# Decay attention, SwiGLU and maxout on one core: the place of a weight's high half in the queues of ScalarE and GpSimd

## The chip, the cores and the metric

The kernel runs on one core of one Trainium2 chip. The metric is the device time of one execution in microseconds (us). The kernel before has a median of 540.08 us over three runs (539.41 to 540.44).

## The reference, cut to what matters

Block-wise linear attention with a decay per head makes x, with 1536 rows of 512. A gated layer and a maxout layer follow. The weights of the two layers are the operands that the change is about.

```python
def _moe_ref(x, w_gate, w_val, w_out, rms_g):
    rms = np.sqrt(np.mean(x * x, axis=-1, keepdims=True) + 1e-06)
    xn = x / rms * rms_g
    g = xn @ w_gate
    silu = g * (1.0 / (1.0 + np.exp(-g)))
    return (silu * (xn @ w_val) @ w_out).astype(np.float32)

def _moe2_ref(x, w1, w2, w3, w_out):
    h = np.maximum(np.maximum(x @ w1, x @ w2), x @ w3)
    return (h @ w_out).astype(np.float32)
```

w_gate, w_val and w_out (512 x 1536, 1536 x 512) arrive as 64-bit floats, and the chip turns them into 32-bit floats itself.

## The kernel before, in words

Every product of the two layers is made of three matmuls: an operand is split into a high half (`xh`, `wh`, `hh`: the value rounded to the type that TensorE reads) and a low half (`xl`, `wl`, `hl`: the value less its high half), and high by high, high by low and low by high are added in PSUM.

The attention runs over 12 chunks of 128 rows. After the first chunks its steps are put between the matmuls of the first layer: transposes of keys and queries (`turn`, L297 and L299) that ScalarE copies out (kT L301, qT L303), scores (L326, with the state's products on L331), mixed values (px L384), their squares (sq L395), a row sum on VectorE (L401), the division by the norm (x L425), the high half of x (xh L427), its low half on GpSimd (xl L435), and a power of -1/2 on GpSimd (diag L414).

A **unit** is one 128x512 slice of a weight matrix: g (gate), v (value) or o (output), with its number. A unit takes three **thirds** for its 32-bit words and then its two halves:

- `begin_unit`: ScalarE makes the absolute high words (L252) and the scaled low words (L253).
- `words_of_unit` 0 to 2: VectorE clamps (L209), masks and shifts (L212) and puts the sign back (L216); GpSimd then adds the low words (L219). Now the tile W holds the 32-bit weight.
- `finish_unit`: ScalarE rounds W to `wh` (L180), GpSimd subtracts to `wl` (L183).

`third_of_unit` (L257) runs one third per call. In a round of three calls it carries one unit's words and finishes the unit before it (`done`): the finish stands in the second call. The matmul loops call it from `spread` and `gap`, after every three matmuls or so.

The **plain part** is the first four slices of the inner dimension, where each product is formed directly (`hidden1`, `out_two`). It runs as long as the list `lates` is empty; `spread` fills that list once the attention has ended. After that comes a part with fewer products, sums of weights and a third call that closes a sum (`later`).

In the plain part the units stand in this order: g0, v0, g1, v1, g2, o0, o1, v2, g3, v3, o2, o3. In the built program the W tiles of those that matter here are numbered W_809 (v1), W_887 (g2), W_958 (o0), W_1037 (o1), W_1176 (v2), W_1229 (g3), W_1376 (v3), W_1426 (o2) and W_1572 (o3).

Each engine takes its instructions in the order in which this code writes them. TensorE's order is that of the matmul loops; a matmul waits for its operands, and those behind it wait with it. SyncE issues the loads.

Of the kernel before, what the change touches and what calls it, by code (L numbers as in the profile page):

```python
# [26 lines left out]
def tile_decay_attention_swiglu_maxout(  # L27
# [41 lines left out]
    lates = []  # L69
# [86 lines left out]
    stage1, stage2 = [], []  # L156
# [17 lines left out]
    def finish_unit(key, W, at):  # L174
        if key:
            if second_sum(key):
                W = sums_in.pop((key[0][1], key[1]))
            wh = wpools[at].tile([P, 512], F32R, tag="wh", name="wh")
            wl = wpools[at].tile([P, 512], F32R, tag="wl", name="wl")
            nc.scalar.copy(out=wh, in_=W.bitcast(F32))  # L180
            if second_sum(key):
                return lambda: lower_of_sum(key, W, wh, wl)
            nc.gpsimd.tensor_tensor(out=wl, in0=W.bitcast(F32), in1=wh.bitcast(F32), op=ALU.subtract)  # L183
            units[key] = (wh, wl)

    def first_sum(key):
        return key and (key[0] == "Tg" or key[0] != "Tv" and key[0][0] == "T" and key[1] % 2 == 0)

    def second_sum(key):
        return key[0][0] == "T" and not first_sum(key)  # L190

    def partner(key):
        return ("v", key[1]) if key[0] == "Tg" else (key[0][1], key[1] + 1)

    def lower_of_sum(key, W, wh, wl):
        nc.vector.tensor_tensor(out=wl, in0=W.bitcast(F32), in1=wh.bitcast(F32), op=ALU.subtract)
        units[key] = (wh, wl)

    def sum_bank(key):
        other = partner(key)  # L200
        sums_in[other] = psum.tile([P, 512], I32, tag="bank", name="tsum")
        nc.scalar.copy(out=sums_in[other].bitcast(F32), in_=words[other].bitcast(F32))

    def words_of_unit(n, key, W, at, lo, hi, split_add=False):

        if key and lo is not None:
            if n == 0:
                mid[key] = W if pos["narrow"] else psum.tile([P, 512], I32, tag="bank", name="mid")
                nc.vector.tensor_scalar(out=mid[key].bitcast(F32), in0=W.bitcast(F32), scalar1=LEAST, scalar2=MOST,  # L209
                                        op0=ALU.max, op1=ALU.min)  # L210
            elif n == 1:
                nc.vector.tensor_scalar(out=mid[key], in0=mid[key], scalar1=0x07FFFFFF, scalar2=3,  # L212
                                        op0=ALU.bitwise_and, op1=ALU.logical_shift_left)
            else:
                if n == 2:
                    nc.vector.scalar_tensor_tensor(out=W, in0=hi, scalar=-0x40000000, in1=mid.pop(key),  # L216
                                                   op0=ALU.bitwise_and, op1=ALU.bitwise_or)
                if n == 3 or not split_add:
                    nc.gpsimd.tensor_tensor(out=W, in0=W, in1=lo, op=ALU.add)  # L219
        elif first_sum(key):  # L220
            if n == 0:
                sum_bank(key)
                return
            a, b = W.bitcast(F32), sums_in[partner(key)].bitcast(F32)
            kept = words[partner(key)].bitcast(F32)
            todo = ((a[:, :HF], b[:, :HF], a[:, :HF]), (b[:, :HF], b[:, HF:], kept[:, :HF]),
                    (b[:, HF:], b[:, HF:], a[:, :HF]), (a[:, HF:], a[:, HF:], b[:, HF:]))
            for o, x, y in todo[2 * n - 2:2 * n]:
                nc.vector.tensor_tensor(out=o, in0=x, in1=y, op=ALU.subtract)

    def begin_unit():
        if pos["made"] == len(unit_list):
            return
        key = unit_list[pos["made"]]
        at = group_of[key] % 2
        if first_use[key] <= pos["step"] + 6 and at < len(wpools) and (key is None or room[at]):
            pos["made"] += 1
            if key is None:
                stage1.append((None,) * 5)
                return  # L240
            room[at] -= 1
            held[key] = at
            if key[0][0] == "T":
                stage1.append((key, None if second_sum(key) else words[key[0][1], key[1]], at, None, None))
                return
            load_to(min(pos["raw"] + 3, 3 * PLAIN + 1) if pos["half"] and not lates else pos["raw"] + (3 if lates else 1))
            pos["raw"] += 1
            t = raws.pop(key).rearrange("p k (f w) -> p (k f) w", w=2)
            lo, hi = t[:, :, 0], t[:, :, 1]
            W = wp.tile([P, 512], I32, tag="W", name="W", bufs=4)  # L250
            words[key] = W
            nc.scalar.activation(out=W.bitcast(F32), in_=hi.bitcast(F32), func=AF.Abs)  # L252
            nc.scalar.activation(out=lo, in_=lo.bitcast(U32), func=AF.Copy, scale=2.0 ** -29)  # L253
            stage1.append((key, W, at, lo, hi))
# [3 lines left out]
    def third_of_unit():  # L258

        if not thirds:  # L260
            if pos["seam"] and stage1 and first_sum(stage1[0][0]):
                return
            done = stage2.pop(0) if stage2 else (None,) * 3
            unit = stage1.pop(0) if stage1 else (None,) * 5
            later = []
            thirds.extend([lambda: (begin_unit(), words_of_unit(0, *unit)),
                           lambda: (later.append(finish_unit(*done)), words_of_unit(1, *unit)),
                           lambda: (later[0] and later[0](), words_of_unit(2, *unit), stage2.append(unit[:3]))])
        thirds.pop(0)()

    xh, xl = {}, {}
# [181 lines left out]
    def gap():  # L453


        pos["gap"] += 1
        if not pos["quiet"]:
            if lates and (pos["step"] == len(steps) or pos["gap"] % 4):
                third_of_unit()
        due.sort(key=lambda e: e[0])  # L460
        while due and due[0][0] <= pos["gap"]:
            due.pop(0)[1]()
        spread()
# [3 lines left out]
    def spread():  # L467
        pos["half"] += 1
        if not lates and (pos["half"] - 1) % 5 % 3:
            third_of_unit()  # L470
        if gaps[0]:
            left = sum(1 for p in attn_q if p[0] <= gaps[1])
            for _ in range(-(-left // gaps[0])):
                attn_step()
            gaps[0] -= 1
            if not attn_q and not lates:
                att_ctx.close()
                wpools.append(ctx.enter_context(tc.tile_pool(name="wp2", bufs=8)))
                lates.append(ctx.enter_context(tc.tile_pool(name="late", bufs=1)))
                pos["narrow"] = False  # L480
                x_sums()
        if pos["half"] == 1:
            finish_unit(*stage2.pop(0))
            words_of_unit(3, *split_unit[0])
# [242 lines left out]
    def unit(at, d):  # L727

        g, i = at
        if i is None:  # L730
            key = ("g", "v", "Tg", "Tv")[d], g
        else:
            key = ("T" if d > 1 else "") + "123"[i], 2 * g + d % 2
        for _ in range(60):
            if key not in units:
                third_of_unit()
        left[key] = left.get(key, (4, 3, 2, 2)[d]) - 1
        if not left[key]:
            mine = units[key]
            free(key)  # L740
            return mine
        return units[key]
# [311 lines left out]
```

## Time and profile before

| what | value |
|---|---|
| median of three runs | 540.08 us |
| the profiled execution's own time | 540.09 us |
| its span, first to last instruction | 538.3 us |
| TensorE matmul busy | 527.4 us, 98% |
| VectorE busy | 370.7 us, 69% |
| GpSimd busy | 301.5 us, 56% |
| ScalarE busy | 279.0 us, 52% |
| mean granted TensorE clock | 0.996 |

All times below are counted from the span's start. The 1.8 us between the span and the execution's time lie around the program. The first attention steps take the stretch up to about 36 us, the plain part of the first layer lies from there to about 161 us, the rest of that layer reaches to about 350 us, and the maxout layer to the end. The weights of the four slices are made before 94 us.

### The profile page before, as it was taken

How to read it: one execution, taken by the hardware profiler on the slowest of the kernel's cores; microseconds unless marked ns; L12 is line 12 of the kernel's file. 1: busy time of each engine (PE TensorE's matmuls, PEld its weight loads, DVE VectorE, ACT ScalarE, POOL GpSimd, SP SyncE). 2: the span in 40 equal slices, each digit the busy share in tenths (PEclk: the TensorE clock that was granted, in tenths of full speed). 3: DMA queues.
4: the chain of work that ended last, by engine and by line, in shares of the span. 5: the costliest groups of instructions: out<-in, count | busy, mean ns of one | idle time of the engine just before them, and what ended most of it. 6: DMA issues, size and time to landing. Idle time of an engine off the chain costs nothing.

```text
span 538.3 us, 9767 instructions
## 1 busy us (share of the span) xinstructions
PE 527.4 (98%) x3728; PEld 435.7 (81%) x3728; DVE 370.7 (69%) x680; ACT 279.0 (52%) x541; POOL 301.5 (56%) x247
## 2 busy tenths in 40 slices
PE   8998999999999999999999999999999999999997
PEld 7776777788888888888888888888888888888886
DVE  5886886549856677857667776878785587684354
ACT  3786774453553774365455446465466745641120
POOL 2487878334345666457365557985387544951060
PEclk9999999999999999999999999999999999999999
DMA  8989563001112213213131221212023321300014
GB/s 194 235 235 251 152 158 81 1 1 39 40 40 79 78 44 113 79 39 89 60 89 39 80 78 40 80 39 64 29 66 120 116 76 43 108 10 0 1 50 185
DMA packets 65598, 44.67 MB, mean 83 GB/s; under 512 B 40080, under 2 KB 61840, under 8 KB 65552
## 3 DMA queue, kind: packets, MB, share of 16 engines
q1 hardware_dynamic: 64848, 44.05, 28.6%
q8 instruction: 29, 0.48, 0.4%
q14 instruction: 17, 0.14, 0.1%
q10 hardware_dynamic: 704, 0.01, 0.1%
HBM read 40.90 MB, written 3.15 MB: 82 GB/s over the span
## 4 chain that ended last, share of the span: by engine, by line
PE 88%; POOL 4%; issue 3%; DMA 2%; DVE 2%; ACT 1%; POOLq 0%; ACTq 0%; DVEq 0%
PE p L691 34%; PE acc L882 9%; PE r L691 9%; PE acc L488 6%; PE acc L489 6%; PE acc L490 6%; PE pv L498 5%; PE q L691 4%; PE pg L498 4%; PE px L384 2%; POOL W L219 1%; DMA wraw<-in_moe_w_val_dram 1%; POOL kd L287 1%; PE pm L410 1%; PE sc L331 1%
## 5 line engine op out<-in xcount | busy, mean ns | idle before, releaser
L183 POOL TENSOR_TENSOR wl<-W,wh 128x512 fp32r<-128x512 f32 x77 | 101.5, 1319 | 51.4 <-ACT wh L180 51.4
L219 POOL TENSOR_TENSOR W<-W,wraw 128x512 int32<-128x512 int32 x60 | 78.9, 1315 | 77.8 <-DVE W L216 77.6
L180 ACT CAST wh<-W 128x512 fp32r<-128x512 f32 x77 | 47.7, 620 | 74.5 <-POOL W L219 73.0
L509 POOL TENSOR_TENSOR hl<-sg,hh 128x512 fp32r<-128x512 f32 x36 | 48.5, 1348 | 38.7 <-ACT hh L508 38.7
L691 PE MATMUL p<-xl,wh 128*128 128x512 f32 x148 | 57.6, 389 | 0.0
L691 PE MATMUL p<-xh,wh 128*128 128x512 f32 x148 | 57.6, 389 | 0.0
L691 PE MATMUL p<-xh,wl 128*128 128x512 f32 x148 | 57.6, 389 | 0.0
L488 PE MATMUL acc<-hh,wh 128*128 128x512 f32 x144 | 56.7, 394 | 0.0
L489 PE MATMUL acc<-hl,wh 128*128 128x512 f32 x144 | 56.2, 390 | 0.0
L490 PE MATMUL acc<-hh,wl 128*128 128x512 f32 x144 | 56.2, 390 | 0.0
L846 DVE TENSOR_TENSOR acc_sb<-acc,acc_sb 128x512 f32<-128x512 f32 x46 | 31.8, 690 | 17.4 <-PE acc L490 16.1
L252 ACT ACTIVATE W<-wraw 128x512 f32<-128x512 f32 x60 | 40.3, 671 | 4.4 <-DMA wraw<-in_moe_w_dram 3.3
L209 DVE TENSOR_SCALAR mid<-W 128x512 f32<-128x512 f32 x58 | 39.7, 685 | 3.3 <-ACT W L252 3.3
L212 DVE TENSOR_SCALAR mid<-mid 128x512 int32<-128x512 int32 x58 | 40.2, 694 | 0.8
L216 DVE SCALAR_TENSOR_TENSOR W<-wraw,mid 128x512 int32<-128x512 int32 x58 | 39.5, 680 | 1.0
L253 ACT ACTIVATE wraw<-wraw 128x512 int32<-128x512 uint32 x60 | 40.0, 666 | 0.0
L746 ACT COPY c<-p 128x512 f32<-128x512 f32 x34 | 19.9, 586 | 38.0 <-PE p L691 37.9
L509 POOL TENSOR_TENSOR hl<-m,hh 128x512 fp32r<-128x512 f32 x18 | 24.2, 1350 | 23.0 <-ACT hh L508 22.9
L508 ACT CAST hh<-sg 128x512 fp32r<-128x512 f32 x36 | 22.3, 620 | 26.3 <-DVE sg L632 18.7
L691 PE MATMUL p<-yh,wh 128*128 128x512 f32 x90 | 35.0, 389 | 0.0
L691 PE MATMUL p<-yl,wh 128*128 128x512 f32 x90 | 35.0, 389 | 0.0
L691 PE MATMUL p<-yh,wl 128*128 128x512 f32 x90 | 35.0, 389 | 0.0
(176 smaller groups left out, 1315.0 us busy)
## 6 DMA issues: line engine op xcount, KB each, us to landing
wraw<-in_moe_w_out_dram SPq DMA_DIRECT2D x18, 512.0 KB, 3.4
wraw<-in_moe_w_dram SPq DMA_DIRECT2D x18, 512.0 KB, 3.5
kn<-in_k_dram SPq DMA_DIRECT2D x12, 256.0 KB, 4.2
qn<-in_q_dram SPq DMA_DIRECT2D x12, 256.0 KB, 5.0
vn<-in_v_dram SPq DMA_DIRECT2D x12, 256.0 KB, 4.5
wraw<-in_moe_w_gate_dram SPq DMA_DIRECT2D x12, 256.0 KB, 3.0
wraw<-in_moe_w_gate_dram SPq DMA_DIRECT2D x24, 128.0 KB, 3.4
wraw<-in_moe_w_val_dram SPq DMA_DIRECT2D x12, 256.0 KB, 3.2
```

The source lines that it names most:

```text
L180: nc.scalar.copy(out=wh, in_=W.bitcast(F32))
L183: nc.gpsimd.tensor_tensor(out=wl, in0=W.bitcast(F32), in1=wh.bitcast(F32), op=ALU.subtract)
L212: nc.vector.tensor_scalar(out=mid[key], in0=mid[key], scalar1=0x07FFFFFF, scalar2=3, op0=ALU.bitwise_and, op1=ALU.logical_shift_left)
L219: nc.gpsimd.tensor_tensor(out=W, in0=W, in1=lo, op=ALU.add)
L252: nc.scalar.activation(out=W.bitcast(F32), in_=hi.bitcast(F32), func=AF.Abs)
L488: nc.tensor.matmul(out=out, lhsT=wh, rhs=xh_, start=first, stop=False)
L489: nc.tensor.matmul(out=out, lhsT=wh, rhs=xl_, start=False, stop=False)
L490: nc.tensor.matmul(out=out, lhsT=wl, rhs=xh_, start=False, stop=last)
L498: nc.tensor.matmul(out=ps, lhsT=w[:, kk * P:(kk + 1) * P], rhs=x[:, kk, :], start=n == 0, stop=n == len(todo) - 1)
L509: nc.gpsimd.tensor_tensor(out=dst_l, in0=src, in1=dst_h.bitcast(F32), op=ALU.subtract)
L691: nc.tensor.matmul(out=ps, lhsT=w[:, ks], rhs=r[:, o + k, :], start=first and k == 0 and n == 0, stop=k == 1 and n == 2, skip_group_check= ...
L882: nc.tensor.matmul(out=acc[:, cs], lhsT=x[:, ts], rhs=w[:, cs], start=n == 0, stop=n == len(todo) - 1)
```

## The change

In the plain part (`lates` empty) the finish of the unit before moves from the second call of a round to the end of the third, behind the words of the round's own unit and so behind their L219 addition. Where `lates` is filled the code does what it did.

```diff
@@ -264,8 +264,9 @@
             unit = stage1.pop(0) if stage1 else (None,) * 5
             later = []
             thirds.extend([lambda: (begin_unit(), words_of_unit(0, *unit)),
-                           lambda: (later.append(finish_unit(*done)), words_of_unit(1, *unit)),
-                           lambda: (later[0] and later[0](), words_of_unit(2, *unit), stage2.append(unit[:3]))])
+                           lambda: (lates and later.append(finish_unit(*done)), words_of_unit(1, *unit)),
+                           lambda: (later and later[0] and later[0](), words_of_unit(2, *unit),
+                                    later or finish_unit(*done), stage2.append(unit[:3]))])
         thirds.pop(0)()
```

The changed kernel has one line more, so lines above 268 count one higher in it. TensorE's, VectorE's and SyncE's orders stay; rows of ScalarE and GpSimd change places.

**First place, ScalarE, at about 48 us.** W_887 is g2; hh is the high half of the first hidden slice; kT and qT are the transposed keys and queries of the next chunk, which TensorE's scores read. Before:

```order
L252 ACTIVATE W_1037<-wraw_952 128x512
L253 ACTIVATE wraw_952<-wraw_952 128x512
L180 CAST wh_1046<-W_887 128x512
L508 CAST hh_1057<-sg_1016 128x512
L301 COPY kT_1081<-pk_1071 128x512
L303 COPY qT_1083<-pq_1072 128x512
```

Of the change:

```order
L252 ACTIVATE W_1037<-wraw_952 128x512
L253 ACTIVATE wraw_952<-wraw_952 128x512
L509 CAST hh_1053<-sg_1012 128x512
L302 COPY kT_1077<-pk_1067 128x512
L304 COPY qT_1079<-pq_1068 128x512
L180 CAST wh_1088<-W_887 128x512
```

The high half of g2 stood ahead of hh, kT and qT, and now stands behind them.

**Second place, GpSimd, at about 58 to 67 us.** W_1037 is o1, whose low half the first output products read; W_1176 is v2. Before:

```order
L219 TENSOR_TENSOR W_1037<-W_1037,wraw_952 128x512
L435 TENSOR_TENSOR xl_939<-x_930,xh_938 128x4x128
L509 TENSOR_TENSOR hl_1220<-sg_1188,hh_1219 128x512
L183 TENSOR_TENSOR wl_1243<-W_1037,wh_1242 128x512
L219 TENSOR_TENSOR W_1176<-W_1176,wraw_954 128x512
```

Of the change:

```order
L219 TENSOR_TENSOR W_1037<-W_1037,wraw_952 128x512
L183 TENSOR_TENSOR wl_1210<-W_958,wh_1209 128x512
L436 TENSOR_TENSOR xl_939<-x_930,xh_938 128x4x128
L510 TENSOR_TENSOR hl_1220<-sg_1188,hh_1219 128x512
L219 TENSOR_TENSOR W_1176<-W_1176,wraw_954 128x512
L183 TENSOR_TENSOR wl_1322<-W_1037,wh_1321 128x512
```

The low half of o1 stood ahead of the addition for v2, and now stands behind it.

**Third place, GpSimd, at about 72 to 95 us.** W_1229 is g3, W_1376 is v3, W_1426 is o2, W_1572 is o3. Before:

```order
L183 TENSOR_TENSOR wl_1457<-W_1229,wh_1456 128x512
L219 TENSOR_TENSOR W_1376<-W_1376,wraw_1172 128x512
L414 TENSOR_TENSOR diag_82<-diag_82,mhalf_79 128x1
L287 TENSOR_TENSOR kd_1577<-kn_1431,Tm_80 128x512
L509 TENSOR_TENSOR hl_1581<-sg_1510,hh_1580 128x512
L183 TENSOR_TENSOR wl_1589<-W_1376,wh_1588 128x512
L435 TENSOR_TENSOR xl_939<-x_1308,xh_938 128x4x128
L219 TENSOR_TENSOR W_1426<-W_1426,wraw_1227 128x512
L183 TENSOR_TENSOR wl_1645<-W_1426,wh_1644 128x512
L219 TENSOR_TENSOR W_1572<-W_1572,wraw_1374 128x512
L509 TENSOR_TENSOR hl_1659<-sg_1633,hh_1658 128x512
L183 TENSOR_TENSOR wl_1757<-W_1572,wh_1756 128x512
```

Of the change:

```order
L219 TENSOR_TENSOR W_1376<-W_1376,wraw_1172 128x512
L183 TENSOR_TENSOR wl_1552<-W_1229,wh_1551 128x512
L415 TENSOR_TENSOR diag_82<-diag_82,mhalf_79 128x1
L288 TENSOR_TENSOR kd_1577<-kn_1431,Tm_80 128x512
L510 TENSOR_TENSOR hl_1581<-sg_1506,hh_1580 128x512
L436 TENSOR_TENSOR xl_939<-x_1304,xh_938 128x4x128
L219 TENSOR_TENSOR W_1426<-W_1426,wraw_1227 128x512
L183 TENSOR_TENSOR wl_1600<-W_1376,wh_1599 128x512
L219 TENSOR_TENSOR W_1572<-W_1572,wraw_1374 128x512
L183 TENSOR_TENSOR wl_1654<-W_1426,wh_1653 128x512
L510 TENSOR_TENSOR hl_1659<-sg_1633,hh_1658 128x512
L415 TENSOR_TENSOR diag_82<-diag_82,mhalf_79 128x1
```

The low half of g3 now follows the addition for v3; that of v3 follows xl and the addition for o2; that of o3 is the row after the last one here, behind the diag of the next chunk, ahead of which it stood.

## Rows read from the trace of the kernel before

**Rows 1.** The page, busy time, share of the span and instructions per engine.

```profile
PE 527.4 (98%) x3728; PEld 435.7 (81%) x3728; DVE 370.7 (69%) x680; ACT 279.0 (52%) x541; POOL 301.5 (56%) x247
```

**Rows 2.** Windows, TensorE: stretch, length, busy (instructions), granted clock, DMA share, GB/s.

```profile
51.00:52.00 1.00, 0.04 (x4) 1.00 1.15 259
53.00:54.00 1.00, 1.00 (x16) 0.50 0.98 285
```

**Rows 3.** Windows: length; PE, PEld, DVE, ACT, POOL busy; clock; DMA share; GB/s.

```profile
16.00:18.00 2.00, 1.07 (x60) 0.94 (x63) 1.29 (x2) 2.00 (x8) 1.06 (x1) 1.00 1.00 248
...
165.00:345.00 180.00, 180.00 (x795) 149.00 (x794) 127.89 (x206) 94.19 (x170) 108.43 (x84) 1.00 0.23 68
```

**Rows 4.** Timeline, TensorE, 49 to 57 us: start, length, what, idle before.

```profile
49.61 0.40 PE L498 MATMUL pg<-xh,wl 128*128 128x512 f32 x1
51.96 0.69 PE L326 MATMUL sc<-qT,kT 64*64 64x64 f32 x32 [1.95 <-ACT qT L303]
...
56.21 0.48 PE L498 MATMUL pv<-xh,wh 128*128 128x512 f32 x1
```

**Rows 5.** Timeline, VectorE (first row) and ScalarE, 47 to 52 us.

```profile
47.16 0.69 DVE L632 TENSOR_TENSOR sg<-pv,sg 128x512 f32<-128x512 f32 x1
...
47.58 0.67 ACT L253 ACTIVATE wraw<-wraw 128x512 int32<-128x512 uint32 x1
49.80 0.62 ACT L180 CAST wh<-W 128x512 fp32r<-128x512 f32 x1 [1.55 <-POOL W L219]
50.32 0.61 ACT L508 CAST hh<-sg 128x512 fp32r<-128x512 f32 x1
...
51.32 0.59 ACT L303 COPY qT<-pq 128x512 f32<-128x512 f32 x1
```

**Rows 6.** Timeline, TensorE, 62 to 67 us.

```profile
62.23 0.46 PE L384 MATMUL px<-qs,S 64*64 64x64 f32 x16
...
63.98 0.69 PE L326 MATMUL sc<-qT,kT 64*64 64x64 f32 x32
...
66.33 0.39 PE L490 MATMUL acc<-hh,wl 128*128 128x512 f32 x1
...
66.70 0.48 PE L488 MATMUL acc<-hh,wh 128*128 128x512 f32 x1
```

**Rows 7.** Timeline, ScalarE (first row) and GpSimd, 58 to 67 us.

```profile
63.08 0.66 ACT L395 ACTIVATE sq<-px 128x256 f32<-128x256 f32 x2 [0.17 <-PE px L384]
...
58.44 0.55 POOL L414 TENSOR_TENSOR diag<-diag,mhalf 128x1 f32<-128x1 f32 x1
...
63.72 1.28 POOL L183 TENSOR_TENSOR wl<-W,wh 128x512 fp32r<-128x512 f32 x1
66.13 1.32 POOL L219 TENSOR_TENSOR W<-W,wraw 128x512 int32<-128x512 int32 x1 [1.13 <-DVE W L216]
```

**Rows 8.** Timeline, TensorE and ScalarE, 72 to 79 us.

```profile
72.69 0.46 PE L384 MATMUL px<-qs,S 64*64 64x64 f32 x16
...
75.01 0.63 PE L326 MATMUL sc<-qT,kT 64*64 64x64 f32 x27 [0.25 <-ACT x L397]
...
78.97 0.39 PE L498 MATMUL pg<-xh,wl 128*128 128x512 f32 x1
...
73.79 0.65 ACT L395 ACTIVATE sq<-px 128x256 f32<-128x256 f32 x2
...
77.71 0.66 ACT L252 ACTIVATE W<-wraw 128x512 f32<-128x512 f32 x1
```

**Rows 9.** Timeline, TensorE, the value product of the fourth slice, v3.

```profile
82.34 0.40 PE L498 MATMUL pv<-xl,wh 128*128 128x512 f32 x1
82.81 0.50 PE L498 MATMUL pv<-xh,wl 128*128 128x512 f32 x1
```

**Rows 10.** Timeline, VectorE and TensorE, the first output product with o3.

```profile
91.43 0.16 DVE L412 TENSOR_SCALAR diag<-pm 128x1 f32<-128x1 f32 x1 [0.42 <-PE pm L410]
...
92.51 0.50 PE L490 MATMUL acc<-hh,wl 128*128 128x512 f32 x1
```

## The prediction

> **What bounds the kernel now.** I read the page's busy line first [rows 1]: TensorE is busy for 98% of the span, GpSimd for 56% and ScalarE for 52%. So only what stops or slows TensorE can move the time. The windows then say where that can be. From 165 us on TensorE is busy for every microsecond at full clock [rows 3]: time lost or won before that is carried to the end, and nothing there can soak it up. The order of the built program differs between about 45 and 95 us alone, so the timeline of that stretch is what counts. Its largest wait of TensorE is the one of 1.95 us at 51.96, for qT [rows 4]. The windows around it show a second price: the granted clock is 1.00 in the idle microsecond and 0.50, the lower of the two levels (1.2 and 2.4 GHz), two microseconds later [rows 2].
>
> All numbers below belong to the profiled execution: 540.09 us, span 538.3, 1.8 us around it. It lies 0.01 us from the median of 540.08, so the sum is put onto 540.09.
>
> **What the change removes.** At 49.80 ScalarE had stood 1.55 us before wh of g2, waiting for GpSimd's addition; hh, kT and qT were queued behind it [rows 5]. With wh behind qT, hh can start when the low words end, about 48.15: its input sg was done at 47.16 + 0.69 = 47.85. From hh's to qT's start took 51.32 - 50.32 = 1.00, so qT starts at 49.15 and ends at 49.74. TensorE's last matmul ends at 49.61 + 0.40 = 50.01, so the scores need not wait: **-1.95 us**. The clock comes on top. From the start of the scores to the first fast matmul took 56.21 - 51.96 = 4.25 us [rows 4]; the same sequence (64 products of scores and state, six wide matmuls, two row sums) took 66.70 - 63.98 = 2.72 us where nothing had stopped TensorE [rows 6]. The difference is **-1.53 us**, and it goes because the idle time that came before it goes.
>
> The busy line alone would price that place otherwise. The window of 53 to 54 us shows TensorE busy for 1.00 of 1.00 us at half clock [rows 2]. The Trainium skill ("Trainium Kernel Development and Optimization", Performance Expectations) says that matmul busy time is a bad metric, because matmuls are pipelined; the trace agrees. By busy time the first place is worth 1.95 us, by the spacing of the matmuls 3.48 us, and the total below would be 1.5 us higher by the former.
>
> **What the change adds.** A weight's low half now stands behind GpSimd's addition for the next weight, and that addition hangs on a long chain that begins at TensorE: px, sq on ScalarE, row sum, division and sign on VectorE, then L219. I follow each low half from sq, so that it doesn't matter how much earlier TensorE runs.
>
> *o1, read by the first output product.* Before, its low half ran from 63.72 to 65.00 and TensorE wanted it at 66.33. Now it follows the addition for v2, which starts 66.13 - 63.08 = 3.05 us after sq [rows 7]. The addition takes 1.28 until the next starts, the low half 1.28, and about 0.05 until TensorE runs: 5.66 us after sq. TensorE wants it 66.33 - 63.08 = 3.25 after sq [rows 6, 7]: **+2.41 us** of waiting. The high half of o1 is late too, behind the cast of xh, but that wait lies within this one.
>
> *g3, read by the gate product of the fourth slice.* Its wh moves into the slot that W's load-side activation had at 77.71 [rows 8]: cast to 78.33, GpSimd 0.07 later for 1.28, 0.05 to TensorE: 79.73, against 78.97: **+0.76 us**. The cast that stood ahead of sq is gone, so sq starts 0.25 sooner after px: 73.79 - 72.69 = 1.10 [rows 8] becomes 63.08 - 62.23 = 0.85 [rows 6, 7]. TensorE's wait of 0.25 for ScalarE's x at 75.01 goes with it: **-0.25 us**; both ends of the g3 wait move alike.
>
> *v3, read by the value product.* On GpSimd the low half of g3, diag, kd, hl, xl and the addition for o2 now all run before it. GpSimd ran those last five, in another order, back to back from 58.44 to 63.72: 5.28 us [rows 7]. From g3's end at 79.68, less 0.03 of overlap, plus 5.28, 1.28 and 0.05: 86.26. TensorE, late by 0.76, wants it at 82.34 + 0.23 + 0.76 = 83.33: a wait of 2.93. Before it paid 82.81 - 82.57 = 0.24 [rows 9]. **+2.69 us.**
>
> *o3, read by the second output product.* Now diag stands ahead of it, which waits for a row sum that TensorE makes just before. VectorE's part ends at 91.43 + 0.16 = 91.59; GpSimd 0.08 later, 0.51 for diag, 1.28 for the low half, 0.05: 93.51, against 92.49 (0.02 of it was paid already) [rows 10]: **+1.00 us.**
>
> g2, o0, v2, o2 and v1 also move, and cost nothing. The closest is g2: its low half ends at about 55.1 and is wanted at 55.3. If that cover is gone it costs tenths. No DMA is issued in another order; the raw buffers that wait for L219 come free earlier, not later.
>
> Sum without clocks: -1.95 - 1.53 - 0.25 + 2.41 + 0.76 + 2.69 + 1.00 = **+3.13 us**.
>
> **Clocks after the new waits.** No row shows a wait of the new shapes. The bounds are the nearest rows: two microseconds with 0.93 idle stayed at 1.00 [rows 3], and 1.95 of idle cost 1.53 [rows 2, 4]. The wait for v3 (2.9 in one piece) lies beyond the upper row, so I take 1.53. The one for o1 is 2.4 in two pieces with two matmuls between; it is nearer to 1.95 than to 0.93, so I take 1.53 again. For g3 and o3 (0.8 and 1.0) I take nothing. With both: 3.13 + 3.06 = +6.2, **546.3 us**.
>
> **The rivals.**
>
> *One new wait keeps the full clock.* For: the two matmuls inside the wait for o1. Against: it is idle for 2.4 of 3 us. 3.13 + 1.53: 544.8 us. If both keep it: 543.2 us. On the first of these, the Trainium skill ("TensorE: Matmul & The Clock Gate", A second HAM failure mode) says that short idle times between groups of matmuls, often repeated, also bring the lower level; by that rule o1's wait pays as well, which is the forecast. Rows 3 speak against it for waits of under one microsecond.
>
> *A third wait pays too.* If g3's or o3's wait, soon after a larger one, finds the clock low again: 546.3 + 1.5 = 547.8 us.
>
> *Faster.* The wait for qT goes and the low halves are in time. GpSimd is idle for 1.13 us before the addition for v2 [rows 7], and if that chain from sq to L219 were shorter by 2.4 us, and v3's queue by 2.9, TensorE would not notice: 540.09 - 3.48 - 0.25, about 536.4 us. The point from which it decides is the start of v2's addition: 0.6 us after sq instead of 3.05. VectorE's order is unchanged, and the row sum, the division and the sign stand in it between the two, so little speaks for it.
>
> *About the same.* The gain of 3.7 us is kept and roughly half of the 6.9 us of new waits is hidden, for instance because v3's queue on GpSimd has room that I don't see: within 1 us of 540.1.
>
> That the change doesn't do what it says is ruled out by the order of the built program.
>
> **How the numbers follow.** About 0.2% (1.1 us) is what a measurement of this kernel can tell from no change. Both clocks fall: 0.45. One falls: 0.24. None: 0.10. A third pays: 0.06. About the same: 0.06. Faster: 0.09. So slower 0.85, same 0.06, faster 0.09. The predicted time is that of the first case, 546.3 us. The range takes in the four slower cases, from 542.5 (no clock lost and 0.7 us less of waiting, some 0.2 per wait) to 548.2 (the third clock and 0.4 more).
>
> **What would show it.** In the changed profile TensorE's scores at about 50 us start without a wait and the granted clock stays at 1.00 there. Four new waits stand on L183's low halves: about 2.4 us in the first output product (with a part on ScalarE's wh), 0.8 in the gate product, 2.9 in the value product, 1.0 in the second output product. Windows at half clock follow the first and the third. The stretch from 165 us on lasts as long as before and only lies later. I am wrong if the low half of o1 starts before the addition for v2, if TensorE waits for v3 under 1 us, or if the scores at 50 us still wait.

## The result, and the profile after

The changed kernel has a median of 546.11 us over six executions (544.42 to 549.4), the kernel before 539.82 us over six beside it (538.31 to 541.13). The ratio is 1.0125 with a 95% interval of 1.009 to 1.0161: slower by 6.3 us, within 0.2 us of the forecast. The profiled execution of the changed kernel took 544.42 us, the shortest of its six, and 4.33 more than the one of before. Both differences have to be accounted for, and they don't have the same parts. Three later executions that lie far outside all others, in a slower state (2992.86 us in E2, 1064.12 in E5, 590.34 in the kernel before beside E1 to E4), are in no median, range or ratio below.

The page's busy line, to be held against [rows 1]:

```profile
PE 529.4 (98%) x3728; PEld 436.7 (80%) x3728; DVE 370.7 (68%) x680; ACT 279.0 (51%) x541; POOL 301.7 (56%) x247
```

Nothing here says that 4.3 us were lost; TensorE's share even stays at 98%. The timeline of TensorE says it. The columns are start, duration, engine, line, operation, and in brackets the idle time before and who ended it:

```profile
49.81 0.69 PE L327 MATMUL sc<-qT,kT 64*64 64x64 f32 x32
...
63.00 0.50 PE L489 MATMUL acc<-hh,wh 128*128 128x512 f32 x1 [0.39 <-ACT wh L180]
...
64.99 0.50 PE L491 MATMUL acc<-hh,wl 128*128 128x512 f32 x1 [1.26 <-POOL wl L183]
...
78.10 0.50 PE L499 MATMUL pg<-xh,wl 128*128 128x512 f32 x1 [0.56 <-POOL wl L183]
...
81.61 0.40 PE L499 MATMUL pv<-xl,wh 128*128 128x512 f32 x1
84.59 0.79 PE L499 MATMUL pv<-xh,wl 128*128 128x512 f32 x1 [2.58 <-POOL wl L183]
...
96.81 0.50 PE L491 MATMUL acc<-hh,wl 128*128 128x512 f32 x1 [0.84 <-POOL wl L183]
```

The scores at 49.81 start without a wait, where [rows 4] had 1.95. Four new waits for low halves stand at o1, g3, v3 and o3, and one for o1's high half (63.00) ahead of that for its low half. The idle times count from a modelled matmul end, 0.39 or 0.40 after its start; against the usual spacing of 0.23 each wait is some 0.17 longer: v3's is 84.59 - 81.61 - 0.23 = 2.75.

GpSimd's timeline shows why each low half is late; [rows 7] is the place of the first two:

```profile
62.40 1.31 POOL L219 TENSOR_TENSOR W<-W,wraw 128x512 int32<-128x512 int32 x1 [1.14 <-DVE W L216]
63.66 1.28 POOL L183 TENSOR_TENSOR wl<-W,wh 128x512 fp32r<-128x512 f32 x1
...
75.21 1.31 POOL L219 TENSOR_TENSOR W<-W,wraw 128x512 int32<-128x512 int32 x1 [3.99 <-DVE W L216]
76.76 1.29 POOL L183 TENSOR_TENSOR wl<-W,wh 128x512 fp32r<-128x512 f32 x1 [0.24 <-ACT wh L180]
...
82.03 1.29 POOL L219 TENSOR_TENSOR W<-W,wraw 128x512 int32<-128x512 int32 x1
83.27 1.27 POOL L183 TENSOR_TENSOR wl<-W,wh 128x512 fp32r<-128x512 f32 x1
...
94.97 0.55 POOL L415 TENSOR_TENSOR diag<-diag,mhalf 128x1 f32<-128x1 f32 x1 [3.50 <-DVE diag L413]
95.48 1.27 POOL L183 TENSOR_TENSOR wl<-W,wh 128x512 fp32r<-128x512 f32 x1
```

Ahead of o1's low half (63.66) stands the addition for v2, and GpSimd is idle for 1.14 us before that, because the addition waits for VectorE's sign. The low half of g3 (76.76) waits 0.24 us for its cast on ScalarE. The one of v3 (83.27) follows the addition for o2 back to back; the one of o3 (95.48) follows a diagonal that came after 3.50 us of waiting.

The windows of the same stretch; the columns are the window, its length, the busy time of PE, PEld, DVE, ACT and POOL, the granted clock, the DMA share and GB/s:

```profile
52.00:54.00 2.00, 2.00 (x12) 1.66 (x10) 2.00 (x8) 1.72 (x4) 2.00 (x3) 1.00 1.01 307
...
64.00:66.00 2.00, 1.01 (x5) 0.90 (x6) 0.38 (x3) 0.56 (x2) 1.06 (x2) 1.00 0.49 151
66.00:68.00 2.00, 2.00 (x10) 1.68 (x9) 1.91 (x6) 1.00 (x3) 2.00 (x3) 1.00 0.92 234
...
85.00:86.00 1.00, 1.00 (x3) 0.75 (x3) 0.10 (x1) 0.00 (x0) 0.82 (x1) 0.50 0.95 254
```

The fall of [rows 2] near 53 us is gone, and behind v3's wait the clock falls to 0.50, the lower of its two levels (1.2 and 2.4 GHz), as forecast. Behind o1's wait it stays at 1.00: here this execution leaves the forecast.

**A ruler.** The first transposes of a chunk's keys (`turn`) are easy to find in every profile, and so is the first product of the maxout layer. Five such rows and that product of the kernel before:

```profile
45.95 0.60 PE L297 MATMUL pk<-ident,kn 128*128 128x128 f32 x4
59.76 0.60 PE L297 MATMUL pk<-ident,kn 128*128 128x128 f32 x4
70.22 0.60 PE L297 MATMUL pk<-ident,kn 128*128 128x128 f32 x4
81.24 0.60 PE L297 MATMUL pk<-ident,kn 128*128 128x128 f32 x4
94.93 0.60 PE L297 MATMUL pk<-ident,kn 128*128 128x128 f32 x4
...
160.94 0.39 PE L691 MATMUL p<-xh,wh 128*128 128x512 f32 x1
```

and of the changed kernel:

```profile
45.83 0.60 PE L298 MATMUL pk<-ident,kn 128*128 128x128 f32 x4
56.04 0.60 PE L298 MATMUL pk<-ident,kn 128*128 128x128 f32 x4
68.96 0.60 PE L298 MATMUL pk<-ident,kn 128*128 128x128 f32 x4
80.50 0.60 PE L298 MATMUL pk<-ident,kn 128*128 128x128 f32 x4
99.19 0.60 PE L298 MATMUL pk<-ident,kn 128*128 128x128 f32 x4
...
165.25 0.39 PE L692 MATMUL p<-xh,wh 128*128 128x512 f32 x1
```

Each difference of two rows is a segment with one of the prediction's places in it. The table has them for every profile taken (E1 to E12 are the experiments below).

| profile | first row at | scores, qT | o1 | x, g3 | v3, o3 | rest | sum |
|---|---|---|---|---|---|---|---|
| before | 45.95 | 13.81 | 10.46 | 11.02 | 13.69 | 66.01 | 114.99 |
| before, E11 | 48.49 | 11.32 | 10.97 | 11.79 | 13.67 | 66.04 | 113.79 |
| before, E12 | 47.03 | 11.29 | 10.98 | 11.80 | 13.70 | 66.05 | 113.82 |
| change | 45.83 | 10.21 | 12.92 | 11.54 | 18.69 | 66.06 | 119.42 |
| change, E8 | 47.39 | 10.21 | 12.95 | 11.56 | 18.52 | 66.05 | 119.29 |
| change, E9 | 44.99 | 10.22 | 14.54 | 11.55 | 18.66 | 66.05 | 121.02 |
| change, E10 | 45.12 | 10.75 | 15.92 | 11.53 | 18.79 | 66.04 | 123.03 |
| E1, four early | 44.79 | 10.22 | 10.68 | 10.74 | 13.74 | 66.08 | 111.46 |
| E2, o1 late | 45.15 | 12.05 | 14.54 | 10.68 | 13.70 | 66.05 | 117.02 |
| E3, v3 late | 48.52 | 11.32 | 10.97 | 11.83 | 17.58 | 66.09 | 117.79 |
| E4, v3 early | 47.88 | 10.22 | 14.51 | 11.56 | 14.72 | 66.05 | 117.06 |
| E5, ahead of add | 45.90 | 10.22 | 13.92 | 11.55 | 18.56 | 66.04 | 120.29 |
| E6, o1, v3 early | 46.87 | 10.22 | 10.45 | 11.64 | 14.76 | 66.06 | 113.13 |
| E7, g2 late | 47.68 | 10.23 | 10.87 | 11.78 | 13.66 | 66.06 | 112.60 |

The last segment is the same in every profile to 0.1 us, and so is the time from the maxout layer's first product to the last one (374.0 to 374.2). What the change does lies in the four segments between. Where the first row stands (44.8 to 48.5) isn't its doing: ScalarE and GpSimd run the same operations on the same tiles in the same order up to v1's low half (46.70 in the kernel before) in all fourteen profiles. In some of them TensorE waits there for loads (1.4 us for vn in E12). In eight the clock falls there, somewhere between 19 and 40 us: in the first profile of the change, in E3 to E8 and in E11. Their first rows stand at 47.3 us on average, those of the other six at 45.5. For the first profile of the change the windows with TensorE alone (length, busy time, granted clock, DMA share, GB/s) show it:

```profile
15.00:20.00 5.00, 4.02 (x110) 0.96 0.90 231
20.00:25.00 5.00, 4.89 (x139) 0.70 0.93 229
```

So the mean clock of an execution counts falls in the start too, and doesn't say by itself which wait had one.

### The profile page after: what moved, and what is told of

Its sections match the earlier page's. It is cut to its first block, busy times and chain, and to the rows that moved or that the text cites. A ratio compares the mean times of both kernels' runs of the same rounds, so it can differ in the third digit from the quotient of the medians.

```text
span 542.6 us, 9759 instructions
## 1 busy us (share of the span) xinstructions
PE 529.4 (98%) x3728; PEld 436.7 (80%) x3728; DVE 370.7 (68%) x680; ACT 279.0 (51%) x541; POOL 301.7 (56%) x247
## 4 chain that ended last, share of the span: by engine, by line
PE 90%; POOL 4%; DVE 2%; issue 2%; DMA 1%; ACT 0%; DVEq 0%; POOLq 0%; ACTq 0%
PE p L692 34%; PE acc L883 9%; PE r L692 9%; PE acc L491 6%; PE acc L489 6%; PE acc L490 6%; PE pv L499 6%; PE pg L499 5%; PE q L692 4%; PE px L385 2%; POOL W L219 1%; POOL wl L183 1%; PE sc L332 1%; PE sc L327 1%; PE pk L298 1%
## 5 line engine op out<-in xcount | busy, mean ns | idle before, releaser
L219 POOL TENSOR_TENSOR W<-W,wraw 128x512 int32<-128x512 int32 x60 | 79.1, 1318 | 81.0 <-DVE W L216 74.9
```

## The experiments

All edits are to the round of three calls. A finish in the second call is called early, one at the end of the third late. In every experiment with an edit but E5 the third call is that of the change, and the second has a condition.

**E1: o1, g3, v3 and o3 early, the others late.**

```diff
-lambda: (later.append(finish_unit(*done)), words_of_unit(1, *unit)),
+lambda: ((lates or done[0] in (('o', 1), ('g', 3), ('v', 3), ('o', 3))) and later.append(finish_unit(*done)), words_of_unit(1, *unit)),
```

> Late finish as in the change, except for o1, g3, v3 and o3, which finish in the second call as before. My theory (the gain at 50 us is real, and the loss is the four waits for these low halves and the clock after them): the gain stands alone, 540.1 - 1.95 - 1.53 - 0.25 = 536.4 us, give or take 0.7, TensorE's scores at 50 us start without a wait, and no wait for a low half is above 0.5 us. Rival (GpSimd as a whole falls behind, whichever weights are late): the waits for o1 and v3 come back because TensorE now arrives 3.5 us sooner, and the time is 539 us or more. Second rival (the early waits are worth nothing, because something later soaks them up): 540 us.

Measured: 535.9 us (535.42 to 536.86), ratio 0.992 (0.9897 to 0.9944). From 45 to 100 us the profile lists no wait of TensorE, and the mean clock is 1.000. Both rivals fall. GpSimd shows why o1 is in time although TensorE comes sooner:

```profile
60.35 1.31 POOL L183 TENSOR_TENSOR wl<-W,wh 128x512 fp32r<-128x512 f32 x1
61.67 1.31 POOL L219 TENSOR_TENSOR W<-W,wraw 128x512 int32<-128x512 int32 x1
```

The low half stands ahead of the addition again. This kernel beats both. Against the change its segments are shorter by 2.2 at o1, 0.8 at g3 and 5.0 at v3 and o3.

**E2: only o1 late** (condition `done[0] != ("o", 1)`).

> Only the finish of o1 is late, all others as before; the wait for qT at 50 us stays. My theory after the changed kernel's trace: the wait for o1 comes in two pieces of together 2.4 us and the granted clock stays at 1.00 behind it: 540.1 + 2.4 = 542.5 us, less up to 0.3 for a wait for x that may go. Rival (the prediction's term: the clock falls there, and the changed kernel's profiled execution was an exception): half clock behind the wait and 544.0 us. Second rival (the low half is in time once TensorE is not ahead): 540.1 us.

Measured: 542.98 us (539.63 to 544.16), ratio 1.0041 (1.0021 to 1.0061): 2.2 us by the ratio, 3.3 by the medians. The waits were 0.69 and 1.25, as in E8 and E9 below. But the granted clock was 0.78 from 66 to 68 us and 0.50 in the window behind:

```profile
68.00:70.00 2.00, 2.00 (x6) 0.50 1.09 257
```

So in this execution my theory that it holds there is wrong, and the prediction's term is back; the wait for qT (1.75) left the clock at 1.00. The median lies between the theory's 542.5 and the rival's 544.0 and decides for neither: the mean clocks of the eleven executions go from 1.000 in two to 0.991 in three.

**E3: only v3 late** (`done[0] != ("v", 3)`).

> Only the finish of v3 is late. On GpSimd its low half then stands behind the low half of x and the addition for o2, but not behind a late g3. My theory: it ends about 2.6 us later than before, 0.24 of it was paid, and the clock falls behind the wait: 540.1 + 2.4 + 1.5 = 544.0 us, with a stretch at half clock near 88 us. Rival (the wait alone, no fall of the clock): 542.5 us. Second rival (the length of v3's wait came from the late low half of g3 ahead of it): a wait of about 1.3 us, 541.3 us.

Measured: 544.53 us (543.4 to 546.7), ratio 1.008 (1.0052 to 1.0108), as the theory had it. The wait stands without a late g3, and the clock is 0.50 from 87 to 89 us. TensorE's row comes first, then GpSimd's, of which the last holds the low halves of v3 and o2:

```profile
86.69 0.80 PE L498 MATMUL pv<-xh,wl 128*128 128x512 f32 x1 [2.54 <-POOL wl L183]
...
84.12 1.29 POOL L219 TENSOR_TENSOR W<-W,wraw 128x512 int32<-128x512 int32 x1
85.36 2.52 POOL L183 TENSOR_TENSOR wl<-W,wh 128x512 fp32r<-128x512 f32 x2
```

The segment grows by 17.58 - 13.69 = 3.9: the wait is 86.69 - 83.75 - 0.23 = 2.71 (the matmul ahead of it starts at 83.75), 0.24 was paid before, and the rest, 1.4, is the clock. The rivals fall.

**E4: all late but v3** (`done[0] == ("v", 3)`).

> The change, except that v3 finishes as before. My theory: v3's term and its clock go, 546.1 - 2.6 - 1.5 = 542.0 us by the medians; by the sum of the waits with no fall of the clock, 540.1 - 1.95 - 1.53 - 0.25 + 2.41 + 0.76 + 0.2 + 1.00 = 540.6 us. If o1's wait costs the clock in most executions: 542.2 us, with half clock behind 65 us in the profile. Rival (the wait for v3 only moves on to the next low half, o2): 544 us or more.

Measured: 540.97 us (539.37 to 544.32), ratio 1.0017 (0.9997 to 1.0037): near the sum without a fall, and the rival falls. In its profile the clock did fall behind o1's wait (0.50 from 68 to 70 us, o1's segment 14.51); that execution took 544.32, the slowest of twelve. Seven of the twelve had a mean clock of 0.999 or more, so in those it can't have fallen. One fall lowers the mean by 0.003 to 0.004 (0.996 with one in the profile of before, 0.993 with two in that of the change, the one near 20 us and the one behind v3, 1.000 with none in E1). E4's profile (0.993) has one behind o1 and one in the start.

**E5: the finish at the head of the third call,** ahead of the addition on GpSimd and where the change has it on ScalarE.

```diff
-lambda: (later and later[0] and later[0](), words_of_unit(2, *unit),
-         later or finish_unit(*done), stage2.append(unit[:3]))
+lambda: ((later and later[0] and later[0]()) if later else finish_unit(*done), words_of_unit(2, *unit), stage2.append(unit[:3]))
```

> The finish moves to the third call as in the change, but stands ahead of that call's words, so GpSimd's low half comes before the addition for the next weight and only ScalarE's place is that of the change. My theory (it is the place one third later that costs, and the addition only for o1): o1's low half starts 0.07 after its wh ends at 62.96 instead of at 63.66, so its wait is 0.6 us shorter; for v3 the addition and g3's low half only change places ahead of it, and its wait stays 2.6 us. 546.1 - 0.6 = 545.5 us. Rival (the additions are what the low halves wait for): 1.3 us less at o1 and 1.3 less at v3, 543.5 us. Second rival (the addition, now later, delays the next diagonal and with it the whole attention): above 547 us.

Measured: 543.54 us (542.17 to 545.38), ratio 1.0067 (1.0039 to 1.0094). The median is the rival's, but the profile isn't:

```profile
63.09 0.50 PE L488 MATMUL acc<-hh,wh 128*128 128x512 f32 x1 [0.70 <-ACT wh L180]
64.45 0.59 PE L490 MATMUL acc<-hh,wl 128*128 128x512 f32 x1 [0.63 <-POOL wl L183]
...
85.67 0.79 PE L498 MATMUL pv<-xh,wl 128*128 128x512 f32 x1 [2.58 <-POOL wl L183]
```

o1's wait is 0.62 shorter and v3's is the same, as the theory said. With a fall behind both, the stretch takes 120.29 against 121.02 in E9: 0.7 less. What else the median gained is probably clock, since two of six executions had a mean of 1.000 and none of the change's; only one of the six was profiled, so this isn't shown.

**E6: the change with o1 and v3 early** (`done[0] in (("o", 1), ("v", 3))`).

> The change, except that o1 and v3 finish as before; of the four costly weights only g3 and o3 are late. My theory (the terms add up, and waits under 1 us leave the clock alone): 535.9 of the first experiment + 0.76 + 1.00 = 537.7 us, a mean clock of 1.00 in most executions. Rival (each new wait costs a clock too): 540.7 us and a clock of 0.994. Second rival (these small waits are soaked up by the following ones): 536 us.

Measured: 539.23 us (537.74 to 542.71), ratio 0.9993 (0.9972 to 1.0013), 1.5 above the expectation and halfway to the first rival's 540.7, so the median alone decides nothing. The stretch is 113.13 - 111.46 = 1.67 longer than in E1, where 1.76 was expected, so the terms do add up; seven of twelve executions had a mean clock of 1.000, so in those the small waits left it alone. In the two profiles the rest lies ahead of the stretch (46.87 against 44.79; E6's has a fall of the clock at 19 to 23 us, E1's has none), where the two kernels have the same order. That the medians differ by more than the stretch for the same reason isn't shown.

**E7: only g2 late** (`done[0] != ("g", 2)`).

> Only the finish of g2 is late, all others as before. My theory (the gain comes from this one weight): 540.1 - 3.48 - 0.25 = 536.4 us, plus up to 1.3 us, because o0's low half then stands right behind g2's late one on GpSimd, ahead of the diagonal and the decayed keys, where the changed kernel has it elsewhere: 536.4 to 537.7. Rival (the gain needs the other weights late as well): 539 us or more.

Measured: 538.45 us (537.61 to 539.79), ratio 0.9973 (0.9956 to 0.999), 0.75 above the upper end, and under the rival's 539. The segment of the scores is 10.23, the whole gain, but TensorE pays 0.33 for qT at 62.52 and 1.00 for x at 74.33 afterwards. So g2 brings the first gain alone. A second one of 1.0 in the segment of x (10.74 in E1) comes, by the rows, from another weight: v2. In the kernel before (E12) GpSimd and ScalarE have, in that segment,

```profile
68.28 1.30 POOL L183 TENSOR_TENSOR wl<-W,wh 128x512 fp32r<-128x512 f32 x1
...
71.80 1.28 POOL L219 TENSOR_TENSOR W<-W,wraw 128x512 int32<-128x512 int32 x1
```

```profile
73.12 0.62 ACT L180 CAST wh<-W 128x512 fp32r<-128x512 f32 x1 [1.61 <-POOL W L219]
73.64 0.65 ACT L395 ACTIVATE sq<-px 128x256 f32<-128x256 f32 x2
```

and in E1 GpSimd and ScalarE have

```profile
66.22 1.32 POOL L219 TENSOR_TENSOR W<-W,wraw 128x512 int32<-128x512 int32 x1
67.49 2.54 POOL L183 TENSOR_TENSOR wl<-W,wh 128x512 fp32r<-128x512 f32 x2
```

```profile
67.78 0.65 ACT L180 CAST wh<-W 128x512 fp32r<-128x512 f32 x1
68.97 0.66 ACT L395 ACTIVATE sq<-px 128x256 f32<-128x256 f32 x2 [0.55 <-PE px L384]
```

In the kernel before, v2's low half (68.28) stands ahead of the addition for g3 (71.80); the cast of g3 waits 1.61 us for that addition, and sq and x stand behind the cast. In E1 the addition comes first, the cast doesn't wait, and sq waits for TensorE alone. No run moved v2 alone, and the wait for x goes in another way too: in E2, where v2 is early, TensorE comes later behind o1's wait and doesn't wait for x (10.68).

**E8: the change again, timed.** **E9 and E10: the change, one execution each.** **E11 and E12: the kernel before, one execution each.** No edit.

> The changed kernel once more, for a second profile and six more executions with their clocks. My theory (the clock falls behind o1's wait in some executions and behind v3's in all; the profiled execution of the changed kernel was one in which it did not behind o1's): median 545 to 547 us, every mean clock at 0.997 or below; the waits are the same 2.4, 0.8, 2.6 and 1.0 us whether the clock falls or not. Rival (the falls belong to the early part of the program and have nothing to do with the waits): executions with a mean clock of 1.00 among the six.

> The changed kernel a third time, for its profile alone: how long it takes from the transposes near 46 us to the first product of the maxout layer, and where the clock falls. My theory: 119.4 us in that stretch if the clock holds behind o1's wait and 120.9 if it falls there (115.0 in the profiled execution of the kernel before); the time before the stretch varies between 44.8 and 48.5 us as it did over ten profiles, whatever the kernel. Rival (what the medians show beyond the stretch is a longer start of the changed kernel): the stretch begins at 47 us or later in the changed kernel and at 46 or sooner in the kernel before.

> The changed kernel a fourth time, for the same: 119.4 us from the transposes near 46 us to the maxout layer without a fall of the clock behind o1's wait, 120.9 us with one; a fall behind v3's wait in any case. Rival: the stretch begins at 47 us or later.

> The kernel before a second time. My theory: the wait for qT is there at 1 to 2 us, and the clock falls behind it in some executions only; the stretch from the transposes near 46 us to the maxout layer takes 115.0 us where it falls, 113.5 or less where it holds, so the change costs up to 6 us against such an execution. Rival (the clock always falls behind this wait): 115.0 us and half clock near 53 us again.

> The kernel before a third time, for the same: 115.0 us in the stretch with a fall of the clock behind the wait for qT, 113.5 us or less without one. Rival: half clock near 53 us in every profile of this kernel.

Measured: E8 546.42 us (543.8 to 546.93), ratio 1.0111 (1.008 to 1.0141), every mean clock at 0.997 or below; E9 545.14, E10 547.26, E11 541.39, E12 540.0, all four beside one more execution of the kernel before, of 541.2. The waits of the change repeat to a few hundredths, except that for o1's high half: 0.39 in the first profile, where the products of the state ahead of it took 0.95 us instead of 0.65, and 0.69, 0.69 and 0.64 in E8 to E10. The clock behind o1's wait doesn't repeat: it held in E8 as in the first profile, and fell in E9, here,

```profile
64.00:66.00 2.00, 1.85 (x7) 1.52 (x8) 1.11 (x3) 0.59 (x1) 1.06 (x3) 0.68 0.80 237
66.00:68.00 2.00, 2.00 (x6) 1.61 (x5) 2.00 (x7) 0.51 (x2) 2.00 (x3) 0.50 1.04 244
68.00:70.00 2.00, 2.00 (x11) 1.54 (x11) 0.04 (x1) 1.34 (x4) 2.00 (x2) 0.97 1.08 245
```

and for longer in E10, here:

```profile
66.00:68.00 2.00, 2.00 (x6) 1.52 (x6) 1.91 (x6) 0.23 (x1) 1.90 (x3) 0.50 0.95 227
68.00:70.00 2.00, 2.00 (x6) 1.61 (x5) 1.11 (x4) 1.10 (x2) 2.00 (x2) 0.50 1.22 275
70.00:72.00 2.00, 2.00 (x8) 1.53 (x8) 0.00 (x0) 0.81 (x2) 1.42 (x2) 0.68 1.03 235
```

By the segment of o1 the fall cost 14.54 - 12.92 = 1.6 us in E9, and 3.0 in E10, whose stretch of 123.03 lies above the 120.9 that was expected. The rival of E9 falls: the stretch began at 45.0 and 45.1 us in the change and at 48.5 and 47.0 in the kernel before. E8's rival falls by its sign, but not wholly: E8's own profile has a fall in the start, at 31 to 35 us, beside the one behind v3. In E11 and E12 the wait for qT was 1.01 and 0.98 us and the clock held:

```profile
52.07 0.69 PE L326 MATMUL sc<-qT,kT 64*64 64x64 f32 x32 [0.98 <-ACT qT L303]
63.06 0.69 PE L326 MATMUL sc<-qT,kT 64*64 64x64 f32 x32 [0.45 <-ACT qT L303]
74.86 0.63 PE L326 MATMUL sc<-qT,kT 64*64 64x64 f32 x27 [1.02 <-ACT x L397]
```

Then the next qT is waited for too, and x for 1.02 instead of 0.25. The first segment is 2.5 us shorter than in the profile of before and the next two are 1.3 longer: the stretch gains 1.2, not 2.5. So the theory of these runs holds, 0.3 us off. E11's mean clock of 0.994 comes from the start, where the clock fell from 29 to 37 us. How long qT is waited for depends on how far TensorE is ahead: from the first row to wh of g2 on ScalarE it is 3.85 us in the profile of before, 3.63 in E2, 2.90 in E11 and 2.87 in E12, and the wait is 1.9 less each time.

## Why the prediction was right, and where it was not

**The wait for qT, -1.95 and -1.53.** Right for the pair of profiles: the segment went from 13.81 to 10.21, -3.60 for -3.48. For the kernel before in general it was too large, because one execution's wait was taken for all. Two of the three profiles of before had half the wait and no fall; against them the change gains only 1.1 there. E2 and E3, with the same order up to that place, waited for 1.75 and 1.01 us, also without a fall.

**The wait for x, -0.25, and g3, +0.76.** Together +0.51; the segment went from 11.02 to 11.54, +0.52. Against E11 and E12 it is 11.54 - 11.80 = -0.26, since the wait for x that goes is 1.02 there. E6 against E1 gives g3 alone in the other variant, +0.90.

**o1, +2.41 and a clock of 1.53.** The wait was right: +2.46 by the segment in the profiled pair. **The step that failed is the clock behind it: "it is nearer to 1.95 than to 0.93, so I take 1.53 again".** It cost 0, 0, 1.6 and 3.0 us in the four profiles of the change. The rival in which one new wait keeps the clock, 544.8 us, is what the first profiled execution did with its 544.42, and E8's too in that stretch. Of seven profiles that have a wait for o1, the clock fell in five. The Trainium skill ("TensorE: Matmul & The Clock Gate", A second HAM failure mode), cited there, speaks of short idle times that recur between groups of matmuls. o1's wait doesn't recur, so "by that rule o1's wait pays as well" went further than the section does, and no run here shows the section's own case.

**v3, +2.69 and 1.53, and o3, +1.00.** 5.22 together; the segment went from 13.69 to 18.69, +5.00. v3's wait was 2.75 (2.93 forecast) and the clock fell behind it in all six profiles that have it. o3 alone is 14.76 - 13.74 = +1.02 by E6 against E1. The queue of v3 was read rightly: in the change GpSimd runs back to back from g3's low half (76.76) to v3's (83.27). But v3 without the late g3 (E3) waits as long: there hl waits for its cast, and xl and the addition for o2 behind it are enough. So the late g3 by itself is not what makes the wait long.

**The sum.** For the profiled pair: +3.13 and one fall make 544.8, measured 544.42. For the medians: the stretch takes 120.7 on average over four profiles of the change and 114.2 over three of before, +6.5, and the medians differ by 6.3 and, in E8, by 7.0. (The same profiled executions as wholes differ by 5.2 only, since the first rows of the change stand 1.3 us earlier on average; that is the start's spread.) By these averages qT and its clock gave 1.8 us and not 3.48, and the new waits, with their clocks and the wait for x, cost 8.3 and not 9.7: o1's clock loss was not there in two executions and was double in one, and the segment of x and g3 is as long as before, where +0.5 was forecast. The two errors, 1.7 and 1.4, nearly cancel. That the forecast of +6.2 came so near the medians is therefore luck in part; that the four waits came out right, and the fall behind v3, is not.

**What stays open:** why the clock falls in one execution behind the same wait and not in the next, and why E1's median lies 3.8 us below that of before when its stretch is only 2.7 shorter than the average of the three. Falls are a part of it: among the executions with a mean clock of 1.000 (three of E1, twelve of before) the medians are 3.2 apart, where the stretch of E1 is 2.4 shorter than that of E12, which had no fall. E1's profile reaches the stretch at 44.8 us, earlier than any other; the early weights, which are late there too, have no part in that, since the order up to there is the same.

## What to carry to other kernels

Moving an instruction back helps what stands behind it and harms what reads it: here one weight (g2) and, by the rows, the addition ahead of v2's low half gained, four weights that are read soon lost, and choosing weight by weight (E1) kept the gain without the loss. Read a queue in order from the instruction that starts it to the reader that wants its end; those four sums came out within 0.2 us of the waits measured. But whether a clock loss follows a wait can be a matter of chance: take several profiles of both kernels before it, or a wait of one execution, goes into a sum, and expect later waits to soak up a part of what it costs or gives back.

## What the runs showed of the hardware

I had taken the length of a wait to decide whether the granted clock falls. It doesn't settle it. Waits for qT left the clock alone at 1.75 us (E2) and lowered it at 1.95 (before). Some 0.69 and 1.25 us for o1 left it at 1.00 in E8 and lowered it in E2, E4, E9 and E10 (0.64 and 1.25 there); 0.70 and 0.63 lowered it in E5. Nor is 0.93 us in two microseconds a safe bound, as the prediction took it from [rows 3]: in the same stretch, 16 to 18 us, TensorE was idle for 0.98 in the first profile of the change and for 0.85 in E6, and from 20 to 22 us both had the clock at 0.50; it was idle for 0.95 in E1, and the clock stayed. v3's wait of 2.5 to 2.6 us lowered it in all six profiles; yet two timed executions of E5 had a mean clock of 1.000. That these falls belong to the waits is shown by the profiles without them: none of the seven without o1's wait and none of the eight without v3's has a fall in that place. And the time at the lower level isn't fixed either: behind nearly the same wait it cost 1.6 us in E9 and 3.0 in E10. In the kernel before, mean clocks from 1.000 to 0.987 stood side by side in 46 executions, which lasted from 538.46 to 543.47 us.
